# Right-hand SBUF pools in another order, and the third early slot's token list read in attention's tail

## The chip, the cores and the metric

One program runs on one core of one Trainium2 chip. The core has five engines that each work through their own queue of instructions in order: TensorE (PE, matrix products and transposes into PSUM), VectorE (DVE), ScalarE (ACT), GpSimd (POOL, which here issues the indirect transfers) and SyncE (SP, which here issues the plain transfers). Semaphores tie the queues together. SBUF is the on-chip memory that operands lie in, PSUM the small memory that PE writes to, and DRAM holds inputs, outputs and two tables that the kernel makes for itself. The metric is device time in microseconds of one execution; lower is better.

## The reference, cut to what matters

Attention with exponential features feeds a mixture of experts in which every token goes to one expert:

```python
def phi(x):
    proj = np.einsum('bhsd,df->bhsf', x, w_phi)
    proj = proj - np.max(np.abs(proj), axis=-1, keepdims=True)
    return np.concatenate([np.exp(proj), np.exp(-proj)], axis=-1)
q_p, k_p = (phi(q), phi(k))
kv = np.einsum('bhsf,bhsd->bhfd', k_p, v)
z = np.sum(k_p, axis=2)
num = np.einsum('bhsf,bhfd->bhsd', q_p, kv)
den = np.einsum('bhsf,bhf->bhs', q_p, z)[..., None] + 1e-06
x = num / den            # (8, 8, 576, 64), then laid out as (8, 576, 512)
...
fresh_e = int(np.argmax(logits[b, s]))
e = fresh_e if s == 0 or local_gate[b, s] < 0.5 else prev_e
h = np.maximum(x[b, s] @ w1[e], 0.0)
out[b, s] = p[e] * (h @ w2[e])     # p: softmax of the logits
```

There are 8 x 576 = 4608 tokens of 512 numbers and 8 experts with weights 512 x 1024 and 1024 x 512. All is computed in float32.

## The kernel before, in words

**Attention.** Two batches of 576 tokens make a stretch `bp` of 1152 tokens, nine chunks of 128; there are four stretches and in each four pairs of heads. Step `p` of the loop (72 steps of two chunks, then a tail) does: `proj(p)`, projections of k and q on PE (L183), their maximum and the difference on DVE, and `kp`, the features of k, on ACT; `qtr(p-1)`, the transposes of q's differences (L203) into the PSUM tile `qt` and the features `qp` on ACT; `kv(p-2)`, the products with v (L225); and a quota of `num`, attention's outputs for a pair of heads that is already summed (L284). `num`'s PSUM tiles (`nm`, two banks) are emptied by DVE (L301 to L308) and written to the DRAM table `xs`, from which tokens are later gathered. `num` is thus the last reader of `qp`; k and q (`kq`), v, `sb` and `kp` are done with when `kv` is.

**Routing.** When a stretch's outputs are complete, `gate(bp)` finds each token's expert and its place among that expert's tokens, and POOL writes token number and probability to the DRAM table `lst` (L510, nine indirect writes of 128 rows). For stretches 1 and 2, `plan_early` then picks early slots: pairs of 128-token units that some expert already has in full. There are three such slots, two after stretch 1 (names ending in `e`) and one after stretch 2 (`f`). `fetch` reads the slot's part of the list (L565, which must wait for every list write before it), transposes it on PE (L577, L578) so that token numbers and probabilities lie along partitions, and copies them on DVE (L579, L580). `gather_x` then has POOL gather the tokens from `xs` into `xg` (L767). For the third slot, `plan_early(2)` issues the list's read as soon as the list is written, and leaves the rest in `self.fetched_last`, which runs as an aside behind layer 1 of the first slot.

**Experts.** `slots` goes through the slots in order. `tokens` transposes a unit (L791) and splits it into a high and a low part (`xhi` on ACT, `xlo` on DVE); `layer1` and `layer2` multiply each by a weight piece that is split in the same way (`whi`, L753, on ACT; `wlo`, L754, on DVE), as three products (L799 to L801). Layer 1's PSUM tiles are emptied by `hh` (L821, ACT) and `hl` (L822, DVE). Weight pieces are loaded by SP (L744) into three raw buffers, and while one slot computes, `spare` loads and splits the pieces of the next. The first slot's eight pieces are loaded and split during attention (`early_weights`). After the three early slots, `plan_main` (its first part an aside of the second slot, its list's transposes behind the third slot's layer 1) plans all that is left, and `moe` runs the main slots.

**Memory.** Pools are stacks on two sides of SBUF. On the right side `front` holds, in the order in which they are opened, `feat` (eight `qp` of 4 KB per partition), `front2` (four `kq` of 3 KB and five `v` of 1.5 KB) and `front3` (three `sb` and four `kp` of 4 KB). When `front` is closed, `open_main` opens `mx2` (36 KB: the early tokens `xhi` and `xlo`, then `hh`, `hl` and `y`) and `w_right` (32 KB: four `whi` and four `wlo`) on the same ground, from the same end. A new pool's first tile waits until everything of the old pools that it lies over has been read. PSUM works in the same way: `psf` holds `pj` and `qt`, and `open_main` puts the experts' tiles over it.

**Order.** In the 72 steps PE's order is that of the code (`manual_schedule`). In the tail, and on the other engines throughout, a planner orders the instructions by the time at which it believes their inputs are there, and among those by a priority: the place in the program, or the first of all within `high_priority`. `issue_after(x)` keeps what it encloses behind `x` on `x`'s engine, in the order alone.

Of the kernel before, what the change touches and what calls it, by code (L numbers as in the profile page):

```python
# [6 lines left out]
F32 = mybir.dt.float32  # L7
# [20 lines left out]
WAIT = 5  # L28
# [18 lines left out]
class Kernel:  # L47
# [9 lines left out]
    def run(self):  # L57
        nc, tc, A = self.nc, self.tc, self.A
        act, dve = self.act, self.dve
        with ExitStack() as root:  # L60
# [24 lines left out]
            back, front = ExitStack(), ExitStack()  # L85
# [1 line left out]
            self.small = self.mkpool(back, "small", 1, "left")  # L87
            self.pskv = self.mkpool(back, "pskv", 1, "left", PSUM)
            self.psb = self.mkpool(back, "psb", 2, "left", PSUM)
            self.feat = self.mkpool(front, "feat", 8, "right")  # L90
            self.front2 = self.mkpool(front, "front2", 2, "right")
            self.front3 = self.mkpool(front, "front3", 3, "right")
            self.psf = self.mkpool(front, "psf", 2, "right", PSUM)
            self.wphases = [(self.moe_early, WE)]

# [3 lines left out]
            n = NBP * NHP * NC  # L99
# [21 lines left out]
            for x in self.background:  # L121
                for _ in x:
                    pass
            front.close()
            self.open_main(root)
            plan = self.plan_main()
            more = lambda: next(plan, None)
            self.slots(self.eslots, {0: lambda: self.fetched_last(), 1: more}, more)
            back.close()
            self.open_rest(root)  # L130
            self.moe()
# [421 lines left out]
    def fetch(self, es, k, n, name, wait):  # L553
# [14 lines left out]
            self.tc.add_manual_dep(ins.ins, x.name, mybir.DependencyInfo(  # L568
                mybir.DependencyClass.Sync, mybir.DependencyReason.DATA), reason="the list is read")
        self.scattered = []  # L570
        for _ in range(wait):
            yield STEP
        t = self.pst([128, 2, n])
        tok = self.psm([128, n], "tok" + name, I32)
        prob = self.psm([128, n], "prob" + name)
        with self.tc.issue_after(self.last_pe.ins):
# [21 lines left out]
    def plan_early(self, bp):  # L598

        dve = self.dve  # L600
        num = HALFWAY if bp == 1 else EARLY - HALFWAY
        nm = "e" if bp == 1 else "f"
        yield STEP
        f = self.floats(self.units_so_far(0, 8, nm), "f" + nm)
# [10 lines left out]
        es, j = self.find(incl, f, self.slote[:, 0:1], nm)  # L615
# [4 lines left out]
        k = self.psm([NU, 1], "k" + nm)  # L620
# [8 lines left out]
        taken = self.psm([NU, E], "tk" + nm)  # L629
        dve.scalar_tensor_tensor(taken, now, 2.0, self.taken, ALU.mult, ALU.add)  # L630
        self.taken = taken
        f = self.fetch(es, k, 2 * num, nm, WAIT)

        def got():
            tok, prob = yield from f
# [372 lines left out]
```

## Time and profile before

| | us |
|---|---|
| median of three runs | 829.67 |
| lowest and highest | 828.54, 830.36 |
| the profiled execution | 827.13 |
| its span, first to last instruction | 825.4 |
| PE busy in the span | 788.1 (95%) |
| DVE, ACT, POOL busy | 555.4, 428.2, 146.7 |

The time of an execution is a little over its span, since starting and ending lie around it. Engines overlap, so the shares add up to more than one. An idle stretch of an engine costs time only where the chain that ends last goes through it; here that is PE nearly everywhere. A row of the timeline is a start, a duration (both in us), engine, line, operation, output and inputs by tile names, shapes and count, and in brackets the idle time of the engine before it with what ended that.

### The profile page before, as it was taken

To read this page: it belongs to the slowest core of one execution; us is meant where nothing else is said; L and a number is where in the kernel's file an instruction comes from. 1 tells how busy PE (TensorE), PEld (TensorE's weight loads), DVE (VectorE), ACT (ScalarE), POOL (GpSimd) and SP (SyncE) were. 2 spreads that over 40 slices of the span, in tenths; PEclk is the share of its full clock that TensorE was granted. 3 is DMA by queue.
4 is the path that set the end of the run, shared out by engine and by line. 5 is a ranking of instruction groups with operands and counts; after the bars stand their busy time and mean duration, and the time that the engine had idled before them with its cause. 6 is when DMAs were issued, how large, how long until landed. Compare 5 with 4: busy or idle time off the path is not lost.

```text
span 825.4 us, 23470 instructions
## 1 busy us (share of the span) xinstructions
PE 788.1 (95%) x9777; PEld 710.0 (86%) x9777; DVE 555.4 (67%) x956; ACT 428.2 (52%) x738; POOL 146.7 (18%) x156
## 2 busy tenths in 40 slices
PE   6999998999989899888999999999999999999997
PEld 5899987898878788777898998998898898999896
DVE  5677897679878885848754444644686777568541
ACT  4666665566666565323543333533564557447431
POOL 0000002200231132051421202212122212201010
PEclk9999999999999999999999999999999999999999
DMA  6545546764799531574974433744696687767510
GB/s 193 141 123 135 144 130 92 124 149 126 151 215 236 168 102 36 157 138 136 393 255 141 162 116 121 286 141 148 207 346 211 209 319 263 257 224 273 192 44 23
DMA packets 74239, 145.01 MB, mean 176 GB/s; under 512 B 9198, under 2 KB 48757, under 8 KB 74112
## 3 DMA queue, kind: packets, MB, share of 16 engines
q1 hardware_dynamic: 66272, 123.14, 50.9%
q0 software_dynamic: 7792, 20.02, 7.2%
q8 instruction: 79, 1.29, 0.7%
q10 hardware_dynamic: 64, 0.30, 0.1%
q14 instruction: 32, 0.26, 0.1%
HBM read 124.51 MB, written 20.26 MB: 175 GB/s over the span
## 4 chain that ended last, share of the span: by engine, by line
PE 69%; issue 12%; DMA 7%; DVE 6%; ACT 2%; POOL 2%; another core or an unknown queue 1%; SPq 1%; POOLq 0%; DVEq 0%; ACTq 0%
PE l L799 12%; PE l L800 12%; PE l L801 12%; PE kvp L225 8%; PE pj L183 8%; PE nm L284 8%; PE qt L203 4%; DMA out<-y,p_tokm 4%; DMA wraw<-in_w2h 2%; PE tr L791 1%; DVE sb L188 1%; DVE m L186 1%; PE nm L263 1%; POOL out L874 1%; DMA p_lrm<-lst,p_rim 1%
## 5 line engine op out<-in xcount | busy, mean ns | idle before, releaser
L753 ACT CAST whi<-wraw 128x1024 fp32r<-128x1024 f32 x160 | 167.5, 1048 | 205.7 <-PE l L801 111.6
L754 DVE TENSOR_TENSOR wlo<-wraw,whi 128x1024 fp32r<-128x1024 f32 x160 | 195.7, 1224 | 85.9 <-ACT whi L753 83.6
L799 PE MATMUL l<-xhi,whi 128*128 128x256 f32 x544 | 155.2, 286 | 2.1 <-DVE hl L822 1.4
L800 PE MATMUL l<-xlo,whi 128*128 128x256 f32 x544 | 152.8, 281 | 0.3 <-DVE xlo L794 0.3
L801 PE MATMUL l<-xhi,wlo 128*128 128x256 f32 x544 | 152.4, 280 | 0.0
L799 PE MATMUL l<-whi,hh 128*128 128x512 f32 x320 | 127.4, 398 | 0.7 <-DVE y L873 0.7
L800 PE MATMUL l<-wlo,hh 128*128 128x512 f32 x320 | 125.8, 393 | 0.0
L801 PE MATMUL l<-whi,hl 128*128 128x512 f32 x320 | 125.7, 393 | 0.0
L186 DVE TENSOR_REDUCE m<-pj 128x8 f32<-128x1024 f32 x72 | 87.9, 1220 | 43.9 <-PE pj L183 43.7
L206 ACT ACTIVATE qp<-qt 128x512 f32<-128x512 f32 x144 | 84.7, 604 | 60.3 <-PE qt L203 57.9
L192 ACT ACTIVATE kp<-sb 128x512 f32<-128x512 f32 x144 | 82.9, 623 | 54.2 <-DVE sb L188 46.5
L799 PEld LDWEIGHTS l<-xhi,whi 128*128 128x128 f32 x544 | 102.8, 189 | 4.5 <-DVE hl L822 1.9
L800 PEld LDWEIGHTS l<-xlo,whi 128*128 128x128 f32 x544 | 102.8, 189 | 1.1 <-DVE xlo L794 0.5
L801 PEld LDWEIGHTS l<-xhi,wlo 128*128 128x128 f32 x544 | 102.9, 189 | 0.0
L284 PE MATMUL nm<-kvs,qp 128*64 128x74 f32 x2304 | 89.0, 230 | 6.8 <-ACT kvs L265 4.8
L183 PE MATMUL pj<-first,kq 64*128 64x128 f32 x1152 | 86.9, 291 | 8.1 <-DMA kq<-in_kqT 6.4
L874 POOL DMA_INDIRECT out<-y,p_tokm x34 | 44.4, 1305 | 269.2 <-DVE y L873 250.7
L188 DVE TENSOR_TENSOR sb<-pj,m 128x1024 f32<-128x1024 f32 x72 | 88.1, 1224 | 3.7
L284 PEld LDWEIGHTS nm<-kvs,qp 128*64 128x64 f32 x2304 | 81.2, 139 | 8.1 <-ACT kvs L265 5.3
L183 PEld LDWEIGHTS pj<-first,kq 64*128 64x128 f32 x1152 | 72.6, 193 | 13.9 <-issue 6.8
L225 PE MATMUL kvp<-v,kp 128*64 128x65 f32 x2048 | 78.1, 227 | 0.5 <-ACT kvs L245 0.4
L225 PEld LDWEIGHTS kvp<-v,kp 128*64 128x64 f32 x2048 | 68.5, 140 | 6.6 <-issue 5.4
(200 smaller groups left out, 1000.3 us busy)
## 6 DMA issues: line engine op xcount, KB each, us to landing
wraw<-in_w1h SPq DMA_DIRECT2D x80, 512.0 KB, 5.9
wraw<-in_w2h SPq DMA_DIRECT2D x80, 512.0 KB, 4.4
kq<-in_kqT SPq DMA_DIRECT2D x47, 384.0 KB, 4.6
v<-in_va SPq DMA_DIRECT2D x48, 195.0 KB, 3.0
xs<-xo SPq DMA_DIRECT2D x48, 128.0 KB, 4.1
xs<-xo SPq DMA_DIRECT2D x16, 192.0 KB, 2.1
vs<-in_va SPq DMA_DIRECT2D x32, 32.5 KB, 3.0
lst<-pr,ri POOLq DMA_INDIRECT x36, 6.3
```

The source lines that it names most:

```text
L183: self.last_pe = self.pe.matmul(t[:, h, i % 2, j, :], kq[r, j, s], self.w2[r], start=True, stop=True)
L186: dve.tensor_reduce(m, f, AX.X, ALU.max, apply_absolute_value=True)
L188: self.last_dve = dve.tensor_sub(sb.rearrange("p h c j f -> p (h c j) f"), f, m.unsqueeze(2).broadcast_to([128, 8, 128]))
L192: self.last_act = act.activation(kp[:, :, :, sg, :].rearrange("p c h f -> p h c f"), sb[:, :, :, 0], AF.Exp, scale=1.0 - 2 * sg)
L206: self.act.activation(qp[:, sg], t, AF.Exp, scale=1.0 - 2 * sg)
L225: self.pe.matmul(self.kvp[r, sg, h], self.ch[i]["kp"][:, h, sg, r], self.v(i, b)[:, h], start=first and n < 2, stop=last and n >= 6)
L284: self.pe.matmul(e["t"][r, c - c0, h, :], self.ch[i]["qp"][:, sg, h, q0 + r.start:q0 + r.stop], kvs[:, sg, h, :], start=sg == 0, stop=sg == 1)
L753: self.act.copy(hi, raw)
L754: self.dve.tensor_sub(lo, raw, hi.bitcast(F32))
L799: mm(o, ah, bh, start=first, stop=False)
L800: mm(o, ah, bl, start=False, stop=False)
L801: self.last_pe = mm(o, al, bh, start=False, stop=last)
```

## The change

Three edits. The first moves `feat` behind `front3` among the right-hand pools. The second takes `fetched_last` from its place behind the first slot's layer 1 and runs it right after the last background step of attention, with the highest priority and before `front` is closed. The third lets `fetch` do this: with `wait` None it borrows the tile `qt` of `psf` for the list's transposes, while before they took a bank of `nm` (`pst` in the tail); `last_pe`, behind which they are kept, is then attention's last projection. The list's read (L565) is issued where it was.

```diff
-            self.feat = self.mkpool(front, "feat", 8, "right")
+
             self.front2 = self.mkpool(front, "front2", 2, "right")
             self.front3 = self.mkpool(front, "front3", 3, "right")
+            self.feat = self.mkpool(front, "feat", 8, "right")
...
+            with tc.high_priority():
+                self.fetched_last()
             front.close()
             self.open_main(root)
             plan = self.plan_main()
             more = lambda: next(plan, None)
-            self.slots(self.eslots, {0: lambda: self.fetched_last(), 1: more}, more)
+            self.slots(self.eslots, {1: more}, more)
...
-        for _ in range(wait):
+        for _ in range(wait or 1):
             yield STEP
-        t = self.pst([128, 2, n])
+        t = self.psf.tile([128, 2, n], F32, name="pt", tag="qt", bufs=1) if wait is None else self.pst([128, 2, n])
...
-        f = self.fetch(es, k, 2 * num, nm, WAIT)
+        f = self.fetch(es, k, 2 * num, nm, WAIT if bp == 1 else None)
```

## The prediction

> **What bounds the kernel now.** I read the stretches first, to see where TensorE (PE) stands idle, then PE's own order around the change, then the queues it waits for.
>
> ```profile
> 335.00:411.00 76.00, 67.83 (x442) 60.17 (x443) 52.92 (x129) 32.18 (x41) 25.89 (x22) 1.00 0.66 200
> 411.00:500.00 89.00, 89.00 (x593) 81.28 (x592) 40.86 (x50) 29.99 (x41) 16.84 (x16) 1.00 0.50 167
> ```
>
> The columns are length, then busy time of PE, weight loads, VectorE (DVE), ScalarE (ACT) and GpSimd (POOL), then clock and DMA. From 411 on PE is never idle, so whatever time PE gains or loses ahead of 411 goes to the end one for one. The 76 us before that hold 8.2 us of idle PE, and the change can only reach these and attention's last 12 us. PE's rows there (start, duration; in brackets the idle time before and what ended it):
>
> ```profile
> 325.58 0.41 PE L263 MATMUL nm<-wgi,ks 128*64 128x18 f32 x8 [0.27 <-DVE rc L301]
> 328.95 1.09 PE L791 MATMUL tr<-first,xg 128*128 128x128 f32 x8
> 330.52 0.41 PE L251 MATMUL nm<-first,kf 128*128 128x128 f32 x2 [0.48 <-DVE rc L301]
> 331.39 0.41 PE L263 MATMUL nm<-wgi,ks 128*64 128x18 f32 x8 [0.46 <-ACT ks L254]
> 332.09 2.79 PE L284 MATMUL nm<-kvs,qp 128*64 128x74 f32 x80 [0.29 <-ACT kvs L265]
> 336.57 0.66 PE L791 MATMUL tr<-first,xg 128*128 128x128 f32 x4 [1.69 <-DVE xlo L794]
> 337.90 0.51 PE L799 MATMUL l<-xhi,whi 128*128 128x256 f32 x2 [0.67 <-ACT xhi L793]
> 338.71 0.38 PE L800 MATMUL l<-xlo,whi 128*128 128x256 f32 x1 [0.30 <-DVE xlo L794]
> ...
> 351.64 0.27 PE L577 MATMUL pt<-first,p_lrf 2*128 2x2 f32 x1
> ...
> 368.70 0.66 PE L791 MATMUL tr<-first,xg 128*128 128x128 f32 x4 [2.27 <-DMA xg<-xs,p_tokf]
> 372.98 0.38 PE L799 MATMUL l<-xhi,whi 128*128 128x256 f32 x1 [0.30 <-DVE hl L822]
> 377.25 0.39 PE L799 MATMUL l<-xhi,whi 128*128 128x256 f32 x1 [1.14 <-DVE hl L822]
> 399.67 0.31 PE L577 MATMUL pt<-first,p_lrm 37*128 37x37 f32 x1 [1.21 <-DMA p_lrm<-lst,p_rim]
> ```
>
> Attention's outputs (L284) end at 334.88. The first early slot's tokens were transposed at 328.95, but their copies out of PSUM come only after that end, and layer 1 runs without gaps from 338.71: 1.69 + 0.67 + 0.30 = 2.66 us of idle. The second idle stretch, 2.27, is the third slot's gather.
>
> ```profile
> 323.26 0.62 ACT L206 ACTIVATE qp<-qt 128x512 f32<-128x512 f32 x1
> 327.59 2.95 ACT L753 CAST whi<-wraw 128x1024 fp32r<-128x1024 f32 x3
> 334.98 1.07 ACT L793 CAST xhi<-tr 128x512 fp32r<-128x512 f32 x2 [2.94 <-PE nm L284]
> 370.01 1.05 ACT L753 CAST whi<-wraw 128x1024 fp32r<-128x1024 f32 x1 [5.79 <-DMA wraw<-in_w1h]
> 370.97 0.59 ACT L821 ACTIVATE hh<-l 128x512 fp32r<-128x512 f32 x1
> ```
>
> **The pool swap.** The third row is what it removes: `xhi` waits for the last reader of `qp` (PE's L284), because its pool lies over `feat`. In the new order `mx2` (36 KB per partition by its tiles) lies over `front2` (20 KB) and part of `front3`, whose last reader is `kv`; the second row shows a tile on that ground being written at 327.59. So the copies can follow the transposes of 328.95, the second unit's transposes (0.66) fall mostly into the 0.46 us gap at 331.39, and layer 1 can follow L284 directly: -2.66, and 0.2 us of transposes that don't fit.
>
> What it adds: `w_right` now lies over `front3` and `feat`, so the three weight pieces of 327.59 wait for the end of L284 instead. That is 2.95 us of ACT, nearly idle then, and three splits on DVE.
>
> ```profile
> 328.68 1.23 DVE L754 TENSOR_TENSOR wlo<-wraw,whi 128x1024 fp32r<-128x1024 f32 x1 [0.21 <-ACT whi L753]
> 329.83 0.42 DVE L306 TENSOR_TENSOR xo<-nm,rc 128x256 f32<-128x256 f32 x1
> ...
> 335.00:340.00 5.00, 2.45 (x17) 2.00 (x18) 4.86 (x20) 1.91 (x4) 0.00 (x0) 1.00 0.73 217
> 340.00:345.00 5.00, 4.98 (x42) 4.60 (x40) 3.82 (x12) 1.55 (x2) 0.00 (x0) 1.00 0.00 0
> 345.00:350.00 5.00, 5.00 (x52) 4.99 (x51) 4.10 (x16) 3.22 (x5) 1.00 (x1) 1.00 0.59 177
> ```
>
> Moving the split of 328.68 out of the way of `xo` frees PE's PSUM bank sooner: the 0.48 at 330.52 goes. But 3 x 1.22 = 3.7 us enters a DVE that is 12.8 of 15 us busy from 335 to 350 (third busy figure), while three `xlo` of 0.68 leave it: 14.4 of 15. The pieces are wanted only by the second slot's layer 1, after 357, so the cover is long; I take 0, and as the other end 2.4 us (two evictions that each wait for a whole split).
>
> **The third slot's list.** Its transposes (0.3 us at 351.64) and gathers move up; the question is where PE meets them and whether the list is there.
>
> ```profile
> 320.51 0.98 POOL L510 DMA_INDIRECT lst<-pr,ri  x1 [0.48 <-DMA lst<-pr,ri]
> 325.40 0.89 POOL L565 DMA_INDIRECT p_lrf<-lst,p_rif  x1 [3.92 <-DMA lst<-pr,ri]
> 348.77 1.00 POOL L510 DMA_INDIRECT lst<-pr,ri  x1 [22.48 <-DVE ri L480]
> ...
> q0 software_dynamic: 31, 0.00, 9.1%
> ...
> q0 software_dynamic: 1, 0.00, 0.1%
> ```
>
> POOL can't read the list before 325.40, as it waits 3.92 us for the last list write. The read's packets (the software queue's, second part) run in 327 to 328, its last one in 328 to 329: landing about 328.7. The diff does not move the read itself. On PE the transposes now have the highest priority, so the planner puts them where it believes the list landed, and in-order PE waits there. It believes too little: the rows at 368.70 and 399.67 show PE standing at a DMA with ready matmuls behind, and in the compiled order of the kernel before, the list's read stands beside PE's last quarter turns, 322.0 in this profile, not 325.4. The same write-to-read step planned again (about 2 us) puts the transposes near 324.3. The earliest place is 323.88, when the bank that they borrow (`qt`) has been read (first ACT row: 323.26 + 0.62). So PE waits from 324.3 to 328.7: 4.4 us, with ends 0 (placed behind the landing) and 4.8. Behind it stand the last `kv`, all remaining L284, and on DVE the `xo` that free PSUM banks, since the two small copies of the list wait in DVE's queue too. This hides the 0.27 at 325.58 and nothing else.
>
> A long wait has a second price, which the clock shows at 145 (row of PE, then stretches with the clock as the last column but two):
>
> ```profile
> 145.38 2.49 PE L284 MATMUL nm<-kvs,qp 128*64 128x74 f32 x36 [3.60 <-ACT kvs L265]
> ...
> 145.00:146.00 1.00, 0.61 (x10) 0.62 (x12) 0.00 (x0) 0.86 (x4) 0.00 (x0) 0.64 1.01 307
> 146.00:147.00 1.00, 1.00 (x22) 1.00 (x20) 0.00 (x0) 1.00 (x4) 0.00 (x0) 0.50 1.18 92
> 147.00:148.00 1.00, 1.00 (x24) 1.00 (x22) 0.22 (x2) 0.41 (x1) 0.00 (x0) 0.50 0.82 35
> 148.00:149.00 1.00, 1.00 (x19) 0.88 (x18) 0.67 (x3) 0.00 (x0) 0.00 (x0) 0.66 0.43 92
> ```
>
> After 3.60 us without work the clock falls to half: 0.36 + 0.50 + 0.50 + 0.34 = 1.7 us lost. I take 1.7 for a wait of 4.4; ends 0 and 1.7. The Trainium skill ("TensorE: Matmul & The Clock Gate", What's actually happening) sets the drop at an idle window of about 3.4 us. By that rule a read placed in the gap at 325.58 would wait 3.1 us and keep the clock, and the sum below would end 3.0 lower.
>
> ```profile
> 246.16 0.93 PE L183 MATMUL pj<-first,kq 64*128 64x128 f32 x10 [1.69 <-issue]
> ...
> 248.00:249.00 1.00, 1.00 (x20) 1.00 (x22) 1.00 (x2) 1.00 (x3) 0.45 (x1) 0.50 0.44 95
> ```
>
> Here the clock was at half after a wait of 1.69 us, so the trace doesn't bear out that limit, and I keep 1.7.
>
> **The gather.** POOL issued it behind nine list writes; now it is done by some 338, in POOL's idle time up to 348.77, and the 2.27 at 368.70 goes. But a wait stands behind it: layer 1's PSUM banks are emptied by `hh` (370.97), which in ACT's order follows a weight piece that waits for its load until 370.01.
>
> ```profile
> 362.70 1.74 SPq L744 DMA_DIRECT2D wraw<-in_w1h  x2
> ...
> DMA to landing us min/median/max: 5.7/5.7/5.7
> ...
> DMA to landing us min/median/max: 8.3/8.3/8.3
> ```
>
> That load took 370.01 - 362.70 = 7.3 us. Weight loads issued from 325 to 350 landed in 5.7, those among the list writes (350 to 365) in 8.3. Attention ends later in the new kernel and its DVE work is denser, so the list writes slide towards this load. At best PE gets all of 2.27 + 0.30 + 1.14 = 3.7, at worst nothing; a load between 5.7 and 7.3 gives up to 1.6, and I take 1.0.
>
> **The sum**, at the third matmul of layer 1 (338.71 before). From 324.3 to 334.88 are 10.58 us with 1.50 idle (0.27, 0.48, 0.46, 0.29); of these 0.46 and 0.29 stay: 9.8 us, plus 0.2 of transposes and two matmuls of 0.12. New: 328.7 + 0.3 (list transposes) + 10.05 + 1.7 + 0.24 = 341.0, which is +2.3. The list transposes missing at 351.64 give -0.3, the gather -1.0: **+1.0 us**. The profiled execution took 827.13 (span 825.4), 2.5 below the median 829.67, so it becomes 828.1, and the median 830.7.
>
> **Rivals.**
> 1. No wait: the transposes land behind 328.7. The same sum without 4.4 and 1.7 is 334.9, or -3.8; with -0.3 and -1.0, -5.1: 824.6. For it: only that the planner's belief is inferred. Against it: the highest priority and the rows at 368.70 and 399.67.
> 2. Wait, but relief: the load lands early enough that all 3.7 go: +2.3 - 0.3 - 3.7 = -1.7: 828.0. For it: half a megabyte of gather leaves the stretch before the load. Against it: the list writes stay there.
> 3. Slower: DVE is the bound in the first slot's layer 1. Place: the `hl` evictions behind the delayed splits; price one split, 1.2, and no relief at the gather: +2.3 - 0.3 + 1.2 = +3.2: 832.9; with two splits +4.4. It decides once DVE has no idle left from PE's restart to the list writes; 14.4 of 15 says that it is close.
> 4. The change doesn't do what it says (tokens still held by another pool's reader, or the read at its old place): about 829.7.
>
> **Chances.** Forecast 0.42, rivals 0.13, 0.15, 0.25, 0.05. What a measurement can tell from no change is 0.2%, 1.7 us. Faster: all of 1, half of 2, a little of the forecast: 0.24. Slower: nearly all of 3 and a quarter of the forecast: 0.33. Same: 0.43. The range 825.3 to 833.8 leaves out the outer part of 1 and of 3; the forecast's own is 829.2 to 832.2.
>
> **What would show it.** Right: the list transposes (p_lrf) among L284 with some 4 us of idle PE before them, ended by the DMA, a clock near 0.5 for 3 us after, `xhi` ahead of L284's end, no gap at 336 to 338, and `whi` x3 behind L284. Wrong: the list transposes behind 328.7 with no gap (rival 1); the rows at 372.98 and 377.25 without idle (2); new idle on PE ended by `hl` in the first slot (3).

## The result and the profile after

| | before | changed |
|---|---|---|
| median, us | 829.11 | 836.85 |
| lowest to highest | 824.65 to 830.36 | 832.24 to 842.39 |
| ratio, with 95% interval | | 1.0097 (1.0070 to 1.0125) |
| the profiled execution, its span | 827.13, 825.4 | 842.39, 840.6 |

The change costs 0.97%, about 8 us. Measured again beside other kernels, the changed kernel was at 836.45 against 830.82: ratio 1.0088 (1.0059 to 1.0117). The forecast was +1.0 us, with a range that ended at 833.8. The profile shown is of the slowest of the first eight executions; the second profile of the changed kernel (832.99 us) is of the fastest of eleven, so the two bracket it.

Single profiles can't be compared from the start of the span. The last projection, which no edit reaches, starts anywhere from 311 to 322 us, for the same kernel too (317.21 and 311.87 in two profiles of the kernel before, 321.62 and 313.51 in two of the changed one). So times are counted below from that start, called P. TensorE's (PE's) rows of the timeline, first of the kernel before (those that stand in the prediction are not repeated):

```profile
317.21 1.16 PE L183 MATMUL pj<-first,kq 64*128 64x128 f32 x16
380.27 0.18 PE L587 MATMUL pt<-cnt,consts 128*37 128x8 bf16 x1
```

and of the changed kernel, whose line numbers are 3 higher from L284 on:

```profile
321.62 1.16 PE L186 MATMUL pj<-first,kq 64*128 64x128 f32 x16
...
331.72 0.25 PE L580 MATMUL pt<-first,p_lrf 2*128 2x2 f32 x1 [2.88 <-DMA p_lrf<-lst,p_rif]
...
342.65 1.09 PE L794 MATMUL tr<-first,xg 128*128 128x128 f32 x8
344.45 0.47 PE L802 MATMUL l<-xhi,whi 128*128 128x256 f32 x2 [0.70 <-ACT xhi L796]
346.47 0.58 PE L803 MATMUL l<-xlo,whi 128*128 128x256 f32 x1 [1.55 <-DVE xlo L797]
...
383.82 0.58 PE L802 MATMUL l<-xhi,whi 128*128 128x256 f32 x1 [5.25 <-DVE hl L825]
392.20 0.58 PE L802 MATMUL l<-xhi,whi 128*128 128x256 f32 x1 [3.59 <-DVE hl L825]
397.51 0.18 PE L590 MATMUL pt<-cnt,consts 128*37 128x8 bf16 x1
...
414.61 0.31 PE L580 MATMUL pt<-first,p_lrm 37*128 37x37 f32 x1
```

Four places can be followed in both. The third matmul of layer 1 (L800, now L803) stands at P + 21.5 before and P + 24.9 after. The small matmul over `cnt` (L587, L590), with which the plan of the main slots begins and which PE reaches at the end of the second slot's layer 1, stands at P + 63.1 and P + 75.9. The transposes of the main slots' list (L577, 399.67 in the prediction's rows, and L580) stand at P + 82.5 and P + 93.0. From there to the end it is 425.7 us before and 426.0 after: what happens later doesn't differ. With the second profile of each kernel (the table below) the means are +3.8 at layer 1's third matmul, +7.0 more by the small matmul, and -1.7 from there to the main list, 9.1 together.

So two idle stretches of the second slot, 5.25 and 3.59 us, have taken the place of 2.27 (the gather), 0.30 and 1.14. The row of ScalarE (ACT) says why, as `hh` must be there before `hl`:

```profile
380.87 1.04 ACT L756 CAST whi<-wraw 128x1024 fp32r<-128x1024 f32 x1 [7.81 <-DMA wraw<-in_w1h]
381.82 0.59 ACT L824 ACTIVATE hh<-l 128x512 fp32r<-128x512 f32 x1
...
389.25 1.04 ACT L756 CAST whi<-wraw 128x1024 fp32r<-128x1024 f32 x1 [2.60 <-DMA wraw<-in_w2h]
390.20 0.59 ACT L824 ACTIVATE hh<-l 128x512 fp32r<-128x512 f32 x1
```

A weight split of the third slot waits 7.81 us for its load, and the eviction of the second slot's first PSUM bank stands behind it. The load itself shows in the list of DMA issues (out<-in, count, size, median us from issue to landing; issues from 364 to 376 us):

```profile
wraw<-in_w1h SPq DMA_DIRECT2D x2, 512.0 KB, 12.6
wraw<-in_w2h SPq DMA_DIRECT2D x1, 512.0 KB, 14.9
lst<-pr,ri POOLq DMA_INDIRECT x9, 7.6
```

12.6 and 14.9 us for the two whose landing is recorded; in the kernel before, the one recorded load among the list writes took 8.3. In the same 12 us GpSimd (POOL) issues the nine list writes of the last stretch, the first and the last of them at

```profile
364.24 0.99 POOL L513 DMA_INDIRECT lst<-pr,ri  x1 [29.44 <-DVE ri L483]
375.45 0.96 POOL L513 DMA_INDIRECT lst<-pr,ri  x1 [0.30 <-DMA lst<-pr,ri]
```

That is P + 42.6 to P + 53.8; before, they went from P + 31.6 (348.77) to P + 42.9. They are 11 us later, 3.4 of them because attention's outputs end 3.4 later (the last L284 starts at P + 17.45, the last L287 at P + 20.88), 0.7 because `g_lt` then follows that end less closely, and 6.9 because the routing takes longer on VectorE (DVE): 12.3 us from `g_lt` (336.43) to the first write before, 19.2 after (14.7 and 19.4 in the second profiles). DVE's rows of the changed kernel:

```profile
343.85 1.23 DVE L757 TENSOR_TENSOR wlo<-wraw,whi 128x1024 fp32r<-128x1024 f32 x1
345.00 0.82 DVE L412 TENSOR_REDUCE g_lt<-lg 128x81 f32<-128x648 f32 x1
345.73 0.68 DVE L797 TENSOR_TENSOR xlo<-tr,xhi 128x512 fp32r<-128x512 f32 x1
346.54 1.22 DVE L757 TENSOR_TENSOR wlo<-wraw,whi 128x1024 fp32r<-128x1024 f32 x1
348.11 1.22 DVE L757 TENSOR_TENSOR wlo<-wraw,whi 128x1024 fp32r<-128x1024 f32 x1
...
351.66 0.28 DVE L437 COPY g_cr<-pt 9x128 f32<-9x128 f32 x1 [1.60 <-PE pt L435]
351.87 1.20 DVE L757 TENSOR_TENSOR wlo<-wraw,whi 128x1024 fp32r<-128x1024 f32 x1
...
363.80 0.16 DVE L483 CAST ri<-g_rf 128x9 int32<-128x9 f32 x1
```

The routing is a chain of some thirty small steps. Of the three splits that the swap has moved, one (343.85) stands just ahead of its first step and two (346.54, 348.11) among its first steps. Four more, where two stood before, come between the later ones, since the chain now runs into them. Each step of the chain that comes behind a split also comes later to PE's transposes and waits for its turn there (1.60).

Idle time is not all of the loss. At layer 1's wait of 1.55 us and at the two stalls, PE's granted clock falls to half (length of the stretch, then busy time of PE, weight loads, DVE, ACT and POOL, the clock, the mean busy share of the DMA engines, and GB/s):

```profile
345.00:350.00 5.00, 3.53 (x18) 3.53 (x19) 5.00 (x16) 1.46 (x3) 0.00 (x0) 0.66 0.62 162
...
383.00:390.00 7.00, 4.79 (x25) 4.47 (x25) 2.59 (x4) 1.80 (x2) 0.00 (x0) 0.76 0.87 143
390.00:400.00 10.00, 7.80 (x35) 7.25 (x36) 6.68 (x10) 4.82 (x7) 0.00 (x0) 0.66 0.27 92
```

The kernel before was at 1.00 from 335 to 500. An account of PE's time shows what this is worth: in each of the 19 profiles that are read here, the time from P to the end is 490.2 to 492.8 us once two things are taken off, idle PE and half of the time that PE works at half clock (the lost clock). The changed kernel's two profiles have 20.4 and 19.4 us of idle PE and 7.4 and 6.7 us of lost clock; those of the kernel before have 15.9 and 15.3, and 0.0 and 4.8. On the mean, 4.3 us of the difference are idle PE and 4.7 are lost clock. The executions of that comparison agree: the median of their mean granted clock is 0.985 for the 11 of the changed kernel and 0.990 for the 34 of the kernel before beside them, by estimate some 4 us of 830.

### The profile page after: what moved, and what is told of

Read it like the earlier page. It is cut to its first block, busy times and chain, and to the rows that moved or that the text cites. A ratio compares the mean times of both kernels' runs of the same rounds, so it can differ in the third digit from the quotient of the medians.

```text
span 840.6 us, 23474 instructions
## 1 busy us (share of the span) xinstructions
PE 793.7 (94%) x9777; PEld 715.1 (85%) x9777; DVE 554.7 (66%) x956; ACT 427.4 (51%) x738; POOL 146.1 (17%) x156
## 4 chain that ended last, share of the span: by engine, by line
PE 67%; issue 12%; DMA 8%; DVE 7%; ACT 3%; POOL 2%; SPq 1%; another core or an unknown queue 1%; POOLq 0%; DVEq 0%; ACTq 0%
PE l L802 12%; PE l L803 12%; PE l L804 12%; PE kvp L228 8%; PE pj L186 7%; PE nm L287 7%; DMA out<-y,p_tokm 4%; PE qt L206 3%; DMA wraw<-in_w2h 2%; DVE m L189 2%; PE tr L794 1%; DVE sb L191 1%; DVE wlo L757 1%; POOL out L877 1%; PE nm L266 1%
## 5 line engine op out<-in xcount | busy, mean ns | idle before, releaser
L802 PE MATMUL l<-xhi,whi 128*128 128x256 f32 x544 | 157.5, 290 | 9.7 <-DVE hl L825 8.8
L803 PE MATMUL l<-xlo,whi 128*128 128x256 f32 x544 | 155.1, 285 | 1.5 <-DVE xlo L797 1.5
L804 PE MATMUL l<-xhi,wlo 128*128 128x256 f32 x544 | 154.6, 284 | 0.0
L803 PE MATMUL l<-wlo,hh 128*128 128x512 f32 x320 | 125.8, 393 | 0.0
L802 PEld LDWEIGHTS l<-xhi,whi 128*128 128x128 f32 x544 | 105.1, 193 | 12.6 <-DVE hl L825 9.8
L195 ACT ACTIVATE kp<-sb 128x512 f32<-128x512 f32 x144 | 82.9, 623 | 52.7 <-DVE sb L191 43.3
L803 PEld LDWEIGHTS l<-xlo,whi 128*128 128x128 f32 x544 | 105.3, 194 | 2.2 <-DVE xlo L797 1.8
L804 PEld LDWEIGHTS l<-xhi,wlo 128*128 128x128 f32 x544 | 105.4, 194 | 0.1
L287 PE MATMUL nm<-kvs,qp 128*64 128x74 f32 x2304 | 90.2, 230 | 5.8 <-ACT kvs L268 3.1
L287 PEld LDWEIGHTS nm<-kvs,qp 128*64 128x64 f32 x2304 | 81.9, 139 | 7.6 <-ACT kvs L268 3.9
L186 PEld LDWEIGHTS pj<-first,kq 64*128 64x128 f32 x1152 | 72.8, 194 | 11.9 <-issue 4.7
```

The lines of the kernel that those rows point to most:

```text
L186: self.last_pe = self.pe.matmul(t[:, h, i % 2, j, :], kq[r, j, s], self.w2[r], start=True, stop=True)
L195: self.last_act = act.activation(kp[:, :, :, sg, :].rearrange("p c h f -> p h c f"), sb[:, :, :, 0], AF.Exp, scale=1.0 - 2 * sg)
L287: self.pe.matmul(e["t"][r, c - c0, h, :], self.ch[i]["qp"][:, sg, h, q0 + r.start:q0 + r.stop], kvs[:, sg, h, :], start=sg == 0, stop=sg == 1)
L802: mm(o, ah, bh, start=first, stop=False)
L803: mm(o, ah, bl, start=False, stop=False)
L804: self.last_pe = mm(o, al, bh, start=False, stop=last)
```

## The experiments

Two theories. **A**: the swap's delayed splits slow the routing, so the last stretch's list writes run among the third slot's weight loads, these land late, and PE stalls. **B**: PE's wait for the third slot's list, and the half clock after it, are the loss. The table gives, for each kernel, the ratio to the kernel before run beside it, and from its profile, in us after P: the third matmul of layer 1, the list writes, the end of the second slot's layer 1 (the matmul over `cnt`), the main list's transposes on PE, and the end. The last columns are of one execution; two profiles of one kernel differ by up to 3 us, so a verdict rests on the ratio and the columns tell where.

| kernel | ratio (95%) | layer 1 | list writes | layer 1, slot 2 | main list | end |
|---|---|---|---|---|---|---|
| before | | 21.5 | 31.6-42.9 | 63.1 | 82.5 | 508.2 |
| before, again (e8) | 1.0001 (0.9966-1.0036) | 21.5 | 33.9-45.3 | 65.7 | 84.0 | 510.9 |
| changed | 1.0097 (1.0070-1.0125) | 24.9 | 42.6-53.8 | 75.9 | 93.0 | 519.0 |
| changed, again (e0) | 1.0088 (1.0059-1.0117) | 25.7 | 43.6-54.9 | 74.4 | 91.7 | 517.6 |
| swap alone (e1) | 1.0040 (1.0010-1.0070) | 20.3 | 39.2-49.8 | 70.2 | 89.6 | 517.0 |
| list alone (e2) | 1.0000 (0.9974-1.0026) | | | | | |
| list alone, again (e11) | 0.9997 (0.9961-1.0032) | 26.1 | 36.1-47.5 | 65.5 | 84.4 | 511.5 |
| swap, list behind outputs (e3) | 1.0012 (0.9984-1.0040) | 20.3 | 36.4-47.8 | 64.6 | 86.1 | 512.7 |
| list behind outputs, old pools (e5) | 1.0011 (0.9980-1.0042) | 25.5 | 37.0-48.4 | 69.3 | 86.7 | 513.2 |
| changed, no list writes (e4) | 1.0002 (0.9977-1.0027) | 24.4 | none | 62.1 | 81.9 | 514.1 |
| e5 with writes later (e7) | 1.0069 (1.0034-1.0104) | 24.5 | 48.7-59.7 | 69.0 | 92.5 | 518.3 |
| changed, routing first (e6) | 1.0067 (1.0035-1.0099) | 26.3 | 44.2-55.4 | 73.1 | 90.2 | 516.6 |
| changed, splits behind routing (e9) | 1.0066 (1.0031-1.0101) | 23.6 | 36.1-47.1 | 72.8 | 93.3 | 519.0 |
| the same, list behind outputs (e10) | 1.0012 (0.9981-1.0044) | 19.3 | 32.0-44.0 | 63.2 | 83.8 | 511.2 |
| changed, splits behind evictions (e12) | 1.0081 (1.0054-1.0108) | 25.2 | 41.7-52.9 | 62.0 | 86.2 | 514.9 |
| the same, list behind outputs (e13) | 1.0015 (0.9987-1.0043) | 20.3 | 36.0-47.4 | 59.6 | 85.6 | 514.3 |
| the same, old pools too (e15) | 1.0055 (1.0031-1.0079) | 24.6 | 35.9-47.3 | 62.0 | 85.6 | 512.6 |
| before, splits behind evictions (e14) | 1.0028 (0.9996-1.0060) | 21.5 | 31.6-42.9 | 61.5 | 86.3 | 515.0 |
| changed, plan first (e17) | 1.0008 (0.9975-1.0042) | 24.9 | 42.9-54.1 | 63.1 | 80.5 | 512.8 |
| the same, list behind outputs (e16) | 0.9998 (0.9968-1.0028) | 20.3 | 36.0-47.3 | 59.5 | 76.8 | 507.8 |

**Each part alone.** The swap alone (the list's part as before), and the list's part alone (the pools in their old order):

```diff
-            with tc.high_priority():
-                self.fetched_last()
...
-            self.slots(self.eslots, {1: more}, more)
+            self.slots(self.eslots, {0: lambda: self.fetched_last(), 1: more}, more)
```

> Only the pool order is changed; the third slot's list is read where it was. Theory A (the swap's delayed weight splits push stretch 3's list writes into the weight loads of the third slot): slower than the kernel before by 3 to 7 us, with the splits of the first three pieces behind the last L284, the list writes starting 5 us or more later than 348.8, and long waits for hl in the second slot's layer 1. Theory B (the loss is PE's wait for the list and the half clock behind it): within 1.7 us of the kernel before, or faster by up to 2.7.

```diff
+            self.feat = self.mkpool(front, "feat", 8, "right")
             self.front2 = self.mkpool(front, "front2", 2, "right")
             self.front3 = self.mkpool(front, "front3", 3, "right")
-            self.feat = self.mkpool(front, "feat", 8, "right")
```

> Only the list's early read; pools in the old order. Theory A: PE's wait of about 3 us and the half clock cost some 3.5, the missing gather wait gives some of it back: between 1 faster and 3 slower. Theory B: slower by 5 to 8, nearly the whole loss.

The second's first profile is of an execution of 4284 us and isn't read; the same kernel was profiled again:

> The list's part alone with the old pools once more, for its profile. Theory A: ratio 1.000 again; TensorE waits about 3 us for the list as in the changed kernel, but the list writes start 14 us or less behind the routing's first step and the third slot's loads take under 9 us, so the second slot's stalls stay under 4 us together and the 2.27 of the gather is gone: the wait is paid back there. Theory B: ratio 1.004 or more.

The swap costs 0.40% by itself, the list nothing, the two together 0.9 to 1.0%. The list's part does make PE wait 2.98 us and brings layer 1 to P + 26.1, 4.5 later than before, but by the end of the second slot's layer 1 it is back at P + 65.5, within the two profiles of the kernel before. Two changes, one free and one at 0.4%, that cost twice the sum: the wait is paid back in the second slot as long as the loads there come in time, and not when the swap has delayed them.

**The list behind the outputs**, with the new pools and with the old: PE reaches the list's transposes after the last output, so it doesn't wait.

```diff
-        with self.tc.issue_after(self.last_pe.ins):
+        with self.tc.issue_after((self.last_num if wait is None else self.last_pe).ins):
```

(`last_num` is the last matmul of L287.)

> As the changed kernel, but the third slot's list transposes are kept behind the last L284, so that PE does not wait for the list. Theory A: 3 to 4 faster than the changed kernel, still 3 to 6 slower than before. Theory B: the loss is gone, within 1.7 us of before or faster.

> The pools as before; the third slot's list is read and its tokens gathered early, as in the changed kernel, but its transposes on TensorE are held behind attention's last output, so TensorE doesn't wait for the list. Theory A (the loss needs the list writes of the last stretch to run among the third slot's weight loads, and the swap's splits on VectorE push them there): with the old pools the list writes start some 32 us after the last projection, as before, the loads are 14 us behind them, and the gather's gap is gone: 1 to 3 us faster than before. Theory B (TensorE's wait and the half clock are the loss): also without loss, 0 to 3 us faster. Set against the list alone (ratio 1.000) it gives the price of the wait: nothing by A, 2 us or more by B.

Without the wait the swap costs 0.12%, no more than can be told from nothing, and with the old pools it is the same 0.11%. Against the list alone (0.00 and -0.03%) the old pools show no price of the wait. With the new pools the price is 0.8 to 0.9%, about 7 us. A wait of 2.9 and 1.7 of lost clock (stretches below) are 4.6, so Theory B alone doesn't explain it. Theory A alone doesn't either: for the swap with the list behind the outputs it expected 3 to 6 us of loss, and the loss was gone, as Theory B had it. The whole loss takes the swap and the wait together. (The gain of up to 3 us that both theories expected with the old pools did not come.)

**No list writes.** The changed kernel without the last stretch's nine writes; its main slots' list lacks that stretch's tokens, so what follows the main list is not comparable.

```diff
-        for c in range(NC):
+        for c in range(NC if bp < NBP - 1 else 0):
```

> As the changed kernel, without the nine list writes of stretch 3 (the tokens of the last 1152 are then not handed to the experts; the main slots do the same work on filler rows). Theory A: the waits of 5.3 and 3.6 us in the second slot's layer 1 shrink to under 2 in sum, 4 to 7 faster than the changed kernel. Theory B: these waits stay, within 2 of the changed kernel.

Rows of PE:

```profile
323.55 0.25 PE L580 MATMUL pt<-first,p_lrf 2*128 2x2 f32 x1 [2.69 <-DMA p_lrf<-lst,p_rif]
...
372.71 0.38 PE L802 MATMUL l<-xhi,whi 128*128 128x256 f32 x1 [0.72 <-DVE hl L825]
...
395.59 0.31 PE L580 MATMUL pt<-first,p_lrm 37*128 37x37 f32 x1
```

The wait is there (2.69), the long stalls are one of 0.72, and the main list is on PE at P + 81.9, ten us earlier than in the changed kernel: the writes decide what the second slot loses. (The ratio of 1.0002 understates it, since what follows takes 6 us longer without that stretch's tokens.) How they do it is seen in stretches of six us at the end of the writes or just behind it (columns as above), of the kernel before

```profile
361.00:367.00 6.00, 5.44 (x32) 4.55 (x30) 4.34 (x4) 2.53 (x3) 2.78 (x4) 1.00 0.57 28
```

of the changed kernel

```profile
371.00:377.00 6.00, 6.00 (x44) 5.55 (x43) 3.62 (x4) 1.71 (x2) 4.78 (x5) 1.00 0.67 37
```

and of the one without list writes

```profile
361.00:367.00 6.00, 6.00 (x42) 5.50 (x41) 4.26 (x5) 3.43 (x4) 1.02 (x1) 1.00 0.62 182
```

The DMA engines are as busy in all three, but they move 28 and 37 GB/s where 182 are possible. The kernel before suffers this too, but there the second slot's layer 1 waits only 0.30 and 1.14 us for `hl`.

**Writes later.** The reverse, from the kernel with the list behind the outputs and the old pools: 40 small copies on POOL ahead of the writes.

```diff
         self.scattering = True
+        if bp == NBP - 1:
+            for _ in range(40):
+                pool.tensor_copy(pr, pr)
```

> The kernel of the list kept behind the outputs with the old pools (e5), with 40 small copies on GpSimd ahead of the last stretch's nine list writes, which makes them some 11 us later, in front of or among the third slot's weight loads. The gather stands ahead of the copies and is not delayed. Theory A: weight pieces arrive 9 us or more after their issue (7.3 before), TensorE stalls 5 us or more in the second slot's layer 1, and the kernel is 3 to 8 us slower than e5. Theory B: the same time as e5 within 1.5 us.

The writes are 11.7 us later after P than in the kernel they are added to, the main list comes 5.8 us later, and the ratio goes from 1.0011 to 1.0069: delaying these writes makes a loss of some two thirds of the change's. Part of it stands at another place than Theory A said: in layer 1 there are 2.44 us that end with `hl` and 1.72 for which the profile names no cause, and 3.81 us in the second layer end with `y`. A run with the copies and without the writes was not made, so a price of the copies themselves isn't excluded.

```profile
387.42 0.39 PE L805 MATMUL l<-xhi,whi 128*128 128x256 f32 x1 [2.44 <-DVE hl L828]
...
401.17 0.80 PE L805 MATMUL l<-whi,hh 128*128 128x512 f32 x1 [3.81 <-DVE y L879]
```

The changed kernel and the kernel before were run once more in this way, with these expectations:

> The changed kernel as it is, once more beside the others. Theories A and B alike: 0.7 to 1.25% slower than before, with the second slot's two stalls of 3 to 5 us again in its profile, since both come from the order of the queues and not from a chance of that one execution. If the stalls were such a chance, the profile would show less than 3 us of them here.

> The kernel before, once more as a kernel of its own: a second profile of it, and what the comparison makes of no change. Theories A and B alike: ratio 1.000 with an interval of about 0.3% to either side, list writes starting 12 us behind the routing's first step, third slot's first three loads taking 7 to 9 us, the same gaps in the second slot (2.3 and 1.1 us).

**Writes earlier, first by priority.** The changed kernel with the last routing at the highest priority.

```diff
-            for _ in self.gate(bp):
-                pass
+            with self.tc.high_priority():
+                for _ in self.gate(bp):
+                    pass
```

> The changed kernel, with the routing of the last stretch (gate(3)) at the highest priority, so that VectorE works through it ahead of the delayed weight splits and the list writes start some 12 us after the routing's first step instead of 19. TensorE's wait for the list and the half clock stay. Theory A: the second slot's layer 1 loses its long stalls (5.25 and 3.59 us in the changed kernel) and the time comes down by 4 to 7 us, to that of before within 0.3%. Theory B: the stalls hardly matter, 1 us or less is gained and it stays about 0.8% slower than before.

The edit doesn't do what it was for. The three splits stand at the same places among the routing's steps (343.18, 345.87 and 347.43 in that profile, `g_lt` at 344.32), and the first write comes 19.4 us after `g_lt`. The planner goes by when it believes an input is there, and only among those by priority. So the ratio, 1.0067 with an interval that holds 1.0088, says nothing of the theories.

**Writes earlier, by order.** The three delayed splits (the ninth to eleventh of the kernel) kept behind the routing's step `g_ef` on DVE, in the changed kernel and with the list behind the outputs.

```diff
+        self.splits = getattr(self, "splits", 0) + 1
+        with self.tc.issue_after(self.routed.ins) if 8 < self.splits <= 11 else nullcontext():
-        self.dve.tensor_sub(lo, raw, hi.bitcast(F32))
+            self.dve.tensor_sub(lo, raw, hi.bitcast(F32))
```

> The changed kernel with the three delayed splits (wlo) held on VectorE behind the last stretch's routing up to its fifth step (g_ef), so that the list writes can start 13 us or less behind the routing's first step (19 in the changed kernel) and stand 10 us or more ahead of the third slot's loads. TensorE's wait for the list and the half clock stay. Theory A: the second slot's two stalls (4.5 and 2.5 us) shrink to 4 us together or less, and 3 to 5 us of the loss of 7.3 come back: ratio 1.003 to 1.005. Theory B: the wait and the half clock are the loss, ratio 1.007 to 1.010.

> As the run before, and the list's transposes held behind attention's last output, so that the wait and the half clock go too: the swapped pools and the early list without the two costs. Theories A and B alike: no loss left, ratio 0.996 to 1.000, and if the swap's own gain of 2.66 us (layer 1 following the outputs without gaps) is real, 0.996 to 0.997; if the second unit's transposes keep standing behind the outputs as in the changed kernel, 0.998 to 1.000.

The chain is mended: 14.0 us instead of 19.2, the last write at P + 47.1, as early as in the kernel with the list alone, which loses nothing. But the ratio is 1.0066, and the second slot has one stall instead of two:

```profile
377.80 0.58 PE L804 MATMUL l<-xhi,whi 128*128 128x256 f32 x1 [10.07 <-DVE hl L827]
```

So Theory A in its first form, in which the place of the writes alone decides, falls. The held-back splits hold their raw buffers longer, so the loads behind them are issued later too (361.06, 364.96 and 369.03 for those that were issued within 2.8 us of each other in the changed kernel). That this keeps the third slot late is likely, but it is not shown by itself. With the list behind the outputs the same edit is at 1.0012, no better than without it; 1.000 or less was expected.

**The queues that the late splits stand in.** What remained open was how late loads become idle PE. In the changed kernel again: the third slot's third to sixth piece are split behind the second slot's evictions that precede them in the program.

```diff
+        self.splits = getattr(self, "splits", 0) + 1
+        with ExitStack() as hold:
+            if 18 < self.splits <= 22:
+                hold.enter_context(self.tc.issue_after(self.last_hh.ins))
+                hold.enter_context(self.tc.issue_after(self.last_hl.ins))
-        self.act.copy(hi, raw)
-        self.dve.tensor_sub(lo, raw, hi.bitcast(F32))
+            self.act.copy(hi, raw)
+            self.dve.tensor_sub(lo, raw, hi.bitcast(F32))
```

> The changed kernel with four weight splits of the third slot (its third to sixth piece, whi and wlo) held behind the second slot's evictions (hh and hl) that come before them in the program; in the changed kernel the first of them stands ahead of the first hh and waits there 7 us for its load. Theory A, by ScalarE's order: the second slot's stalls (4.5 and 2.5 us, with half clock after each) go, and the time comes down by 5 us or more, to a ratio of 1.003 or less, list wait and all. Theory A, by the lateness of the loads alone: the stall moves to the second slot's second layer or the third slot and the ratio stays above 1.006. Theory B (the list wait is the loss): 1.006 or more.

The same edit with the list behind the outputs, in the kernel before, and with the list behind the outputs and the old pools:

> Swapped pools, the list's transposes behind attention's last output, and the third slot's four splits behind the second slot's evictions: no wait, and late loads stop no eviction. Theory A by ScalarE's order: faster than before, ratio 0.992 to 0.998 (3.1 us of stall in the second slot go from a kernel at 1.001). Theory A by lateness alone, and Theory B: 1.000 to 1.003 as without the edit.

> The kernel before with only the four splits held behind the second slot's evictions. Of its idle time in the second slot 2.3 to 3.2 us wait for the third slot's gather and stay, 0.3 and 1.1 end with hl and go: by Theory A with ScalarE's order ratio 0.997 to 1.000, by Theory B 1.000.

> As the run of e13 with the pools in the old order: what the swap itself is worth once neither the list's wait nor the late loads stop TensorE. Theory A by ScalarE's order: ratio 0.995 to 0.999, up to 2.7 us slower than with the swap if the swap's gain at the first slot's start is kept to the end, equal if it is taken back. Theory B: 1.000 to 1.002.

Both stalls are gone from the changed kernel's second slot: its layer 1 ends at P + 62.0 instead of 74.4 to 75.9. And nothing that can be told from zero is gained, 1.0081. Some of the time has moved to the next place, PE at the main slots' list:

```profile
405.44 0.33 PE L580 MATMUL pt<-first,p_lrm 37*128 37x37 f32 x1 [6.94 <-DMA p_lrm<-lst,p_rim]
```

In DVE's rows of this kernel the plan of the main slots runs from `p_um` to `p_rim`, with the late splits between its steps:

```profile
381.40 0.16 DVE L592 TENSOR_SCALAR p_um<-pt 37x8 int32<-37x8 f32 x1 [0.46 <-PE pt L590]
382.86 1.23 DVE L762 TENSOR_TENSOR wlo<-wraw,whi 128x1024 fp32r<-128x1024 f32 x1
...
391.47 1.23 DVE L762 TENSOR_TENSOR wlo<-wraw,whi 128x1024 fp32r<-128x1024 f32 x1 [0.54 <-ACT whi L761]
394.19 0.75 DVE L881 TENSOR_SCALAR y<-l,p_probe 128x512 f32<-128x512 f32 x1
395.46 0.15 DVE L563 TENSOR_SCALAR p_rim<-p_rowm 37x1 int32<-37x1 f32 x1
```

14 us for a chain of some forty steps of 0.15 to 0.2 us, which takes 9 in the kernel before. The clock falls to half at PE's 6.94 us too (3.1 us lost by the account above). The other three kernels show the same wait: 8.72, 7.46 and 6.32 us. In the kernel before, the edit thus turns 1.2 us at the main list into 7.46 and is not faster (1.0028). With the list behind the outputs the old pools are at 1.0055 and the new ones at 1.0015, the one place where the swap seems worth something, some 3 us (the intervals overlap). All four expectations by ScalarE's order were wrong in the gain and right in the stalls that go.

**Plan first.** So in the last two, the third slot's splits from its third piece on are also kept behind `p_rim` on DVE (L563; `listed` is that step), and the calls that make them come behind the plan in the program.

```diff
-            if 18 < self.splits <= 22:
+            if 18 < self.splits <= 24:
                 hold.enter_context(self.tc.issue_after(self.last_hh.ins))
-                hold.enter_context(self.tc.issue_after(self.last_hl.ins))
+                hold.enter_context(self.tc.issue_after(self.listed.ins))
...
-            have = [0]
+            have, most = [0], [2 if i == 1 and 1 in asides else 8]
...
                 asides[i]()
+            if most[0] < 8:
+                most[0] = 8
+                spare(4)
+                spare(4)
```

> The same edit in the changed kernel, whose wait for the third slot's list (3 us and the half clock) stays. If late loads cost time only through the two queues, the loss goes: 6.9 us at the main slots' list shrink to 3 or less, ratio 0.996 to 1.002, about 0.5% above the run beside it (the wait). If the wait itself or something else is the loss, 1.005 or more.

> Swapped pools, the list's transposes behind attention's last output, and the third slot's splits from its third piece on behind the second slot's evictions on ScalarE and behind the main slots' plan (its last step, p_rim) on VectorE; their loads are issued later too. If late loads cost time only through these two queues, the 8.7 us at the main slots' list shrink to 3 or less and the kernel is faster than before, ratio 0.990 to 0.997. If the third slot then waits for its weights, a stall of 3 us or more stands in its layers and the ratio is 0.998 to 1.004.

The changed kernel's rows of PE:

```profile
324.84 0.24 PE L580 MATMUL pt<-first,p_lrf 2*128 2x2 f32 x1 [2.98 <-DMA p_lrf<-lst,p_rif]
...
395.10 0.31 PE L580 MATMUL pt<-first,p_lrm 37*128 37x37 f32 x1
...
424.56 0.39 PE L807 MATMUL l<-xhi,whi 128*128 128x256 f32 x1 [2.10 <-DVE hl L830]
```

The loss is gone: 1.0008 (0.9975 to 1.0042), with the swap, the 2.98 us of wait and the list writes at P + 42.9 to 54.1, as late as in the changed kernel. The loads of the third slot's third to fifth piece are still issued among them, at P + 50.2 to 53.0 (49.9 to 52.7 in the changed kernel); the later ones come at P + 73.0 and on instead of P + 61.6. No wait stands at the main list (P + 80.5). So what the list writes cost the changed kernel, they cost through the two queues in which late splits stood ahead of `hh` and of the plan. One doubt is left: the edit was not run in the kernel before, and a gain that it would bring to any kernel counts here as loss undone. With the list behind the outputs it is worth 0.14% (0.9998 against 1.0012), which speaks against a large gain of that kind.

Of the 11 to 13 us by which the main list comes earlier, 6.4 are given back behind it (432.3 us to the end instead of 425.9). Of PE's idle time there, 0.69 and 0.82 us end with the gather of main slots' tokens and 2.10 with `hl` in a main slot's layer 1; the changed kernel has none of the three, and what makes them is not traced further. Without PE's wait for the list 0.990 to 0.997 was expected and 0.9998 measured. So no version of this study is measurably faster than the kernel before.

**The wait and the swap, over all pairs.** With the swapped pools, holding the list behind the outputs takes the ratio from 1.0097 and 1.0088 to 1.0012, from 1.0066 to 1.0012 and from 1.0081 to 1.0015, that is by 4.5 to 7 us, and only in the last pair by nothing that can be told from zero (1.0008 and 0.9998). PE's wait is thus a part of the loss, as Theory B said, but, as far as these ratios tell, not with the old pools, and not where late splits hold up neither evictions nor the plan.

## Why the prediction was wrong

Predicted +1.0 us, measured +7.3 to +8.0 by the two ratios, +9.1 at the main list by the mean of two profiles. What failed are three terms: the swap's gain of 2.66, the three delayed splits on DVE at 0, and the gather at -1.0 with nothing as its worst. Step by step:

**The wait: right, smaller.** PE stood at the list's transposes among L287, ended by the DMA, for 2.88 and 3.22 us; the sum had 4.4. PE came there at P + 7.2, the forecast's place (324.3 is P + 7.1), and the list landed 1.1 to 1.4 us sooner after P than taken.

**The half clock: right behind the wait, left out behind it.** The stretches behind the wait:

```profile
331.00:332.00 1.00, 0.28 (x2) 0.31 (x2) 0.00 (x0) 0.00 (x0) 0.00 (x0) 1.00 0.02 2
332.00:333.00 1.00, 1.00 (x23) 0.99 (x24) 0.86 (x4) 0.00 (x0) 0.44 (x1) 0.73 0.00 0
333.00:334.00 1.00, 1.00 (x24) 1.00 (x22) 0.31 (x2) 0.00 (x0) 0.69 (x2) 0.50 0.23 71
334.00:335.00 1.00, 1.00 (x22) 1.00 (x22) 0.59 (x3) 0.19 (x1) 0.80 (x1) 0.50 0.84 175
335.00:336.00 1.00, 1.00 (x26) 1.00 (x24) 0.00 (x0) 0.12 (x1) 0.00 (x0) 0.56 0.86 246
```

0.27 + 0.50 + 0.50 + 0.44 = 1.7 us, as taken. It fell behind 2.88 us without work. The sum has no such term for any other wait.

**The swap's -2.66: failed.** Two `xhi` do come ahead of attention's end (339.14 and 340.09 on ACT), as forecast. But from the start of the last output to layer 1's third matmul it is 3.97 us, and 4.06 before. The prediction saw that "the copies can follow the transposes" and put the second unit's transposes into a gap; they stand behind all of L287 (342.65), their first `xhi` behind a `whi` (343.73), their `xlo` behind a `wlo` and `g_lt` (345.73 behind 343.85 and 345.00). The two edits of the swap meet: what waits for the same end of L287 and is ahead in the queue is the three pieces that the swap has moved there. So layer 1 is late by 3.3 and 4.2 us, not 2.3. The swap alone shows the same: layer 1's third matmul is 1.2 us earlier there (P + 20.3), and 1.1 of it is that the outputs end earlier, at P + 16.6 instead of P + 17.7. With 2.9 and 1.7 us for the wait and its clock that makes +3.4.

**Three splits on DVE at 0: failed.** The other end, 2.4, was thought of at the evictions. It was the routing that paid, 12.3 to 19.2 us, and its last step releases the list writes. The prediction named the cover for the splits ("wanted only after 357"), and did not ask who stands behind them on DVE.

**The gather's -1.0: the step that decides.** "At best PE gets all of 3.7, at worst nothing." The sentence before it has the cause: the list writes slide towards this load. Its price was left with a floor of nothing, though the same rows gave it: a load among list writes took 8.3 us instead of 5.7, and behind it stood `hh`. Measured: the gather's 2.27 is gone, and 0.30 + 1.14 of waiting for `hl` are 5.25 + 3.59. From layer 1's third matmul to the main list the forecast was -1.3, the mean of two profiles is +5.4: 6.7 of the 8 us by which the sum was short. By the account above, this part is worse by 3.1 us of idle PE and 3.2 of lost clock; the prediction had a floor of zero for the first and nothing for the second.

**The rivals.** Rival 3 had the sign, half of the size (+3.2, or +4.4 with two splits) and the right engine, DVE behind the delayed splits, but the wrong victim. The no-wait rival is out, as PE waited. The change did what its edits say.

**What stays open.** Why small writes slow the loads beside them is not shown, only that they do. That the wait costs nothing with the old pools fits the second slot's slack, but that the slack is the cause was not tried. In the last two kernels the wait makes 5 us between the profiles (1.5 of idle PE and 3.4 of lost clock) and 0.1% between the ratios, which the intervals don't settle. The plan-first edit in the kernel before is missing. Why holding the splits back behind the routing brought so little is argued, not tried.

## What to carry to other kernels

When a change moves the end of a chain, price the chain's last transfer at its new place, among the transfers that it then meets, and not only the chain's own engine. For every load that can be late, list what stands behind the instruction that waits for it, on each engine: here an eviction on one engine and a planning chain on another were held by the same late weights, and mending one only moved the stall to the other. Count the granted clock behind every wait and not idle time alone; here it was half of the loss. Two edits that are free or cheap alone must be priced together where one uses up the slack that hides the other.

## What the runs showed of the hardware

The list writes are the surprise. Each carries 128 rows of 8 bytes, in 16 packets of 64 bytes, and yet while they land some 4 KB packets of the weight loads, and of the gather beside them, take microseconds. After 340 us the median of such a packet is 0.16 us in every kernel; in the kernel before 40 of 23,303 took more than 1.5 us, up to 4.4, and 35 of these lie between 352 and 367 us, with the writes issued from 348.77 to 360.13. Without those writes only 3 did, none before 727 us. Packets that slow also occur during attention, where the earlier stretches' writes are spread; which of them belong to a write was not followed. The Trainium skill ("DMA: Bandwidth & Descriptors", Specifications) says that transfers below 512 B are done as read-modify-write, which would fit a write that is dear for its size; of the transfers beside it that table says nothing. The Trainium skill ("DMA: Bandwidth & Descriptors", Back-pressure in remote DMA) has it that stalled writes stall the other queues of their DMA engine, there for transfers between cores; the traces here agree in what they show, 28 GB/s at a busy share of 0.57, but no run shows the mechanism.

The clock fell to half behind 2.88 us without work, less than the 3.4 us that the Trainium skill ("TensorE: Matmul & The Clock Gate", What's actually happening) gives; the prediction had drawn on a row of 1.69 us for the same. And 2.27 us (368.70 in the kernel before) left it at 1.00, so in these traces the length of the idle time alone doesn't decide.
